# A fused attention and two-MLP kernel: order of the first softmaxes, one weight slice kept on the core, and the pace of two background preparations

## The chip, the cores and the metric

One Trainium2 chip, one of its cores. The metric is the time of one execution in device microseconds; the median of several executions counts. Five engines work side by side, each through its own queue: TensorE (PE in the profile; its weight loads are PEld), VectorE (DVE), ScalarE (ACT), GpSimd (POOL) and SyncE (SP), which here issues all DMA transfers.

## What is computed

Packed attention, then two MLPs over its result, in float32. Batch 8, 8 heads, 576 tokens, head size 64, 32 packing queries; width 512, inner widths 2048 and 1024.

```python
def sm_attn(q, k, v):
    s = q @ k.T / sqrt(64)
    a = exp(s - max(s)); a = a / (sum(a) + 1e-9)
    return a @ v
p_packed = sm_attn(p, k, v)                 # 32 rows a head
x = sm_attn(q, p_packed, p_packed)          # 576 rows a head; heads side by side: 4608 x 512
h = maximum(x @ w_in, 0)                    # 4608 x 2048
y = (h * h) @ w_out                         # 4608 x 512
h = y @ w_in2                               # 4608 x 1024
solu = h * softmax(h)
ln = (solu - mean(solu)) / sqrt(var(solu) + 1e-6) * g_ln
out = ln @ w_out2                           # 4608 x 512
```

The four weight matrices come as float64 and are turned into float32 on the core.

## The kernel before

**Products.** A float32 product is made of three passes of a faster format (`fp32r`): each operand is split into a rounded high part (a ScalarE copy) and the rest (`split_lo`, line 66, a subtraction on VectorE or GpSimd), and high x high, low x high and high x low are added in PSUM.

**First stages (`t` = 0 to 9).** `K0` is a `Pack` (line 164): it computes the packed attention of batches 0 to 3 for one head after the other. `scores` (197), `soft` (212), `transp` (236, which brings the exponentials through PSUM into `eT`; two copies a head, by turns on VectorE and ScalarE), `packed` (248), and `pairs` (262), which leaves for each pair of heads the packed values in `slc` and, split, in `L`. Batches 4 to 7 follow much later as a second `Pack` inside the steps.

**The first MLP's input weights, per batch.** The attention's last product is merged into the weights: a `Unit` (289) takes a 256 x 256 block of `w_in` (slice `s` of 8, head group `g` of 2), decodes it (`Decode`, 119: a ScalarE activation at line 136 and three VectorE instructions at 141, 147 and 149), splits it (`fin`, 295) and multiplies it by `L` (`product`, 304). The result `pw` is split into `pws` (320, 321), stored to DRAM (`store`, 340), and read back batch by batch as a `slot` (`load_slot`, 350). For batch 0 and slices 0 and 1, `product` first calls `first` (325): it computes batch 0's quarter once more by itself (`pd`) and writes the slot straight from PSUM, so that no way over DRAM is needed. `wout_unit` (354) decodes a chunk of `w_out` in the same manner into `woh` and `wol`.

**The second softmax.** `s2_jobs` (367) makes for a batch and a head group the list of jobs that end in `at` (`ah`, `al`): load of the query, scores `s`, transposes, max, subtraction, exponential, sum, normalization, transpose back, split. For batches 0 and 1 VectorE does all but exponential and high copy. For batch 0's group 1 the list comes in two halves of 288 tokens (`parts` = 2), for the others in one.

**Steps.** From `t` = 10 on (`T0`; step `i` = `t` - 10) the main loop (932) runs 256 steps, one for a batch, a half of its tokens and one of 16 chunks of the inner width: `h1` (445) multiplies `slot` by `at` (6 matmuls), ScalarE applies relu and squares, VectorE splits into `ghl`; three or four steps later `ymm` (475) multiplies by `wo` into four PSUM banks `Y` (12 matmuls). The first 32 steps alternate between batches 0 and 1 in blocks; slice `s` serves chunks `2s` and `2s + 1`, so batch 0 needs slice 2 at step 16 and slice 3 at step 18. Beside that, `at_step` (518) holds a table of jobs for each step: loads of slots, begin and decoding of units (`unit_at`, 529; `wout_at`, 541), softmaxes of later batches, the second `Pack`, its units, and from step 137 on the preparation of the second MLP.

**Preparation of the second MLP.** It runs by Strassen-Winograd with seven instead of eight block products (`strassen`, 830). The weights' seven operands are made by `quads` (635) from decoded units (`wi_unit`, `wx_unit`), one unit every `PD` = 5 steps, and stored to DRAM (`wi_d`, `wx_d`). The seven operands of each of the first 14 pairs of token tiles are made by `pre_y` (753), one pair every `RD` = 6 steps from step 138 on, and stored to `yc_d`. At step `t0` = 230 the buffers of these preparations close (`to_w2`, 584), and the operands come back: `load_wi` (591), `fetch_y` (808), and from step 244 on `load_wx` (597) into the buffers that `wo` leaves free. `h2(0)`, the first product of the second MLP, stands at step 249.

**What sets the order.** Matmuls by `mm` and all DMAs are issued in the program's order. The instructions of VectorE, ScalarE and GpSimd are ordered by the framework's scheduler, by the program's order and by its own estimate of when they are ready, except where they are pinned: by `pin`, or, while `strict[0]` is set (steps 138 to 245), all of them.

Of the kernel before, what the change touches and what calls it, by code (L numbers as in the profile page):

```python
# [27 lines left out]
NPRE = 14  # L28
# [8 lines left out]
def build(tc, qT, kT, vP, pT, w_in, w_out, w_in2, w_out2, g_ln, out):  # L37
# [25 lines left out]
    def dma(out, in_):  # L63
        pin(SP.dma_start(out=out, in_=in_))
# [99 lines left out]
    class Pack:  # L164
# [71 lines left out]
        def transp(self, n):  # L236
            t = self.pl.tile([P, KC * P], F32, tag="eT", name="eT", bufs=2) if self.own else t25("2", "eT")
            self.eT[n] = t.rearrange("p (k c) -> p k c", k=KC)
            for a, b in ((0, 3), (3, KC)):
                pt = bank("pt")[:, :(b - a) * P]  # L240
                for c in range(a, b):
                    flip(self.own, pt[:, (c - a) * P:(c - a + 1) * P], self.e1[n % 2][:, c * P:(c + 1) * P], ident)
                if next(TURN["ETC"]) == "A":
                    A.copy(t[:, a * P:b * P], pt)
                else:
                    V.tensor_copy(t[:, a * P:b * P], pt)
# [28 lines left out]


    wo, slot = {}, {}
    T0 = 10
    ring, clock = [0], [0]
    later, soons, lows = [], [], []  # L280

    def soon(fn):
        if strict[0]:
            soons.append(fn)
        else:
            fn()


    class Unit:
        def __init__(self, bg, s, g, pl, bufs):  # L290
            self.bg, self.s, self.g, self.pl, self.done = bg, s, g, pl, False
            self.d = Decode(pl, w_in.rearrange("(k p) c -> p k c", p=P)[:, 2 * g:2 * g + 2, s * 512:(s + 1) * 512],
                            (2, 256), self.fin, bufs)

# [9 lines left out]

        def product(self):
            bg, s, g = self.bg, self.s, self.g
            if bg == 0 and s < 2:
                self.first()
            t = [bank("pw") for _ in range(2)]
            for j in range(2):  # L310
                c = slice(j * 256, (j + 1) * 256)
                for i, (a, x) in enumerate(((0, 0), (1, 0), (0, 1))):
                    for hh in range(2):
                        r = slice(64 * hh, 64 * hh + 64)
                        mm(t[hh][:, c], L[bg, 2 * g + j][r, a, :], self.w[r, x, c], start=(i == 0), stop=(i == 2))
            sb = self.pl.tile([P, 4, 2, 2, P], F32R, tag="pws", name="pws", bufs=2)
            for hh in range(2):
                o = sb.rearrange("p (j h) c l x -> p h j c l x", h=2)[:, hh]
                src = t[hh].rearrange("p (j c x) -> p j c x", j=2, c=2)
                pin(A.copy(o[:, :, :, 0], src))  # L320
                V.tensor_tensor(out=o[:, :, :, 1], in0=src, in1=f(o[:, :, :, 0]), op=ALU.subtract)
            later.append(lambda: self.store(f(sb.rearrange("p h c l x -> p h (c l x)"))))


        def first(self):
            s, g = self.s, self.g
            if (0, s) not in slot:
                new_slot(0, s)
            t = bank("pd")[:, :256]
            for j in range(2):  # L330
                for i, (a, x) in enumerate(((0, 0), (1, 0), (0, 1))):
                    for hh in range(2):
                        r = slice(64 * hh, 64 * hh + 64)
                        mm(t[64 * j + 32 * hh:64 * j + 32 * hh + 32], f(L[0, 2 * g + j][r, a, :32]),
                           f(self.w[r, x, j * 256:(j + 1) * 256]), start=(i == 0), stop=(i == 2))
            o, src = slot[0, s][:, g], t.rearrange("p (c x) -> p c x", c=2)
            pin(A.copy(o[:, :, 0], src))
            V.tensor_tensor(out=o[:, :, 1], in0=src, in1=f(o[:, :, 0]), op=ALU.subtract)

        def store(self, sf):  # L340
            bg, s, g = self.bg, self.s, self.g
            for b4 in range(bg == 0 and s < 2, 4):
                r = slice(32 * b4, 32 * b4 + 32)
                dma(pw_d[4 * bg + b4, s, :, g].rearrange("(h p) c -> p h c", h=4), sf[r])

# [172 lines left out]
    def at_step(i, fn):  # L518
        jobs.setdefault(i if i == "first" else T0 + i, []).append(fn)

# [44 lines left out]
                i = max(i, 9 + 24 * s // 5)  # L565
            at_step(base + i, lambda b=b, s=s: load_slot(b, s))
    for s, (i, k) in enumerate(((None, 4), (None, 6), (11, 12), (15, 16), (25, 26), (29, 30), (39, 40), (43, 44))):
        if i:
            at_step(i, lambda s=s: load_slot(0, s))
        at_step(k, lambda s=s: load_slot(1, s))  # L570

# [125 lines left out]
        unit_at(P2 + 1 + u * 12 // 5, 1, u // 2, u % 2, lambda: X["p"], (3, 2, 2))  # L697
    p1 = P2 + 1 + 36 + 9
    at_step(p1, open_prep)
    PD = 5  # L700
    for u in range(16):
        mk = (lambda u=u: wi_unit(u // 4, u % 4)) if u < 8 else (lambda u=u: wx_unit((u - 8) // 2, u % 2))
        decode_at(p1 + 1 + PD * u, mk)
    t0 = 230
    assert p1 + 1 + PD * 15 + 6 <= t0
    at_step(t0, lambda: W2["dst"].close())
    at_step(t0, lambda: X["yst"].close())
# [39 lines left out]
        return {"11": yl[:, :, :P], "12": yr[:, :, :P], "21": yl[:, :, P:], "22": yr[:, :, P:]}  # L747


    R0, RD = 138, 6  # L750
    assert R0 + RD * (NPRE - 1) >= 213 > R0 + 5 * RD >= 101

    def pre_y(m):
        i0 = R0 + RD * m
# [53 lines left out]
    def fetch_y(i):  # L808
        m = ORDER[i]
        c = places(i)  # L810
        if m < NPRE:
            for j, n in enumerate(AO):
                dma(f(c[n]), yc_d[m][:, j])
            ytl[i] = {n: halves(t) for n, t in c.items()}
            return
        ytl[i] = {n: halves(t) for n, t in c.items()}
        y2 = [p2.tile([P, 2, 256], F32, tag=f"yf{k}", name="yf", bufs=1) for k in range(2)]
        for k in range(2):
            dma(y2[k], y_d[:, 2 * k:2 * k + 2, m * 256:(m + 1) * 256])
        for js in operands(quadrants(*y2), lambda n: (*ytl[i][n], lambda: None), lambda n: V if n in ("22", "12") else G):  # L820
            for fn, *x in js:
                fn(*x)
# [76 lines left out]
        W2["yst"].close()  # L899

    for i in range(2):
        at_step(t0 + 4 + 6 * i, lambda i=i: fetch_y(i))
    for i in range(14):
        at_step(t0 + 1 + i, lambda i=i: load_wi(i))
    at_step(249, lambda: h2(0))


    K0 = Pack(0, era, False)
# [9 lines left out]
    ps1 = {}  # L918
    early = {}
    done = [0]  # L920
    q0 = {}

    def load_q(g):
        if g == 0:
# [7 lines left out]
    for t in range(max(max(j for j in jobs if j != "first"), T0 + N + LAG - 1) + 2):  # L932
        i = t - T0
        clock[0] = t
        if not 1 <= i <= 3:
            for fn in later:
                fn()
            later.clear()
        for n in ((0,), (1,), (2,), (3,), (4, 5), (6, 7))[t] if t < 6 else ():
            K0.load_v(n)  # L940
        if t + 3 < H:
            K0.load_k(t + 3)
        if t + 1 < H:
            K0.scores(t + 1)
        if t == 3:
            load_q(0)
        if t == 5:
            load_q(1)
            for j in jobs.pop("first"):
                j()  # L950
        if t == H:
            ps0_st.close()
            ps1["p"], ps1["st"] = pool("ps1", space=PSUM)
            Y += [ps1["p"].tile([P, HF], F32, name=f"Y{o}") for o in range(4)]
        if 0 <= t - 1 < H:
            K0.transp(t - 1)
        if t + 1 < H:
            K0.soft(t + 1)
        if 0 <= t - 2 < H:
            K0.packed(t - 2)  # L960
        if t in (4, 6, 8, 9):
            K0.pairs(t // 2 - 2 if t < 9 else 3)
        if t < 9:
            products()
        if t == 6:
            for j in s2_jobs(0, 0, q0[0]):
                j()
        if t == 9:
            early[0] = s2_jobs(0, 1, q0[1], 2)
            for j in early[0][:2]:  # L970
                j()
            products()
            for j in early[0][2:9]:
                j()
            open_b()
            early[1] = s2_jobs(1, 0), s2_jobs(1, 1)
            for x in early[1]:
                x.pop(0)()
            x, y = early[1]
            early[1] = x[:4] + [j for z in zip(x[4:], y) for j in z] + y[len(x) - 4:]  # L980
        strict[0] = R0 <= i < 246
        sq = None
        if 0 <= i < N:
            sq = h1(steps[i])
        for fn in soons:
            fn()
        soons.clear()
        if sq and not strict[0]:
            sq[0]()
            sq[1]()  # L990
        for j in jobs.get(t, ()):
            j()
        if sq and strict[0]:
            sq[0]()
        for fn in lows:
            fn()
        lows.clear()
        if sq and strict[0]:
            lows.append(sq[1])
        products()  # L1000
        if i == 0:
            for j in early[0][9:]:
                j()
        if 1 <= i < 6:
            for j in early[1][4 * i - 4:4 * i]:
                j()
        while done[0] < N and done[0] <= i - lag(i):
            ymm(steps[done[0]])
            done[0] += 1
# [120 lines left out]
```

## Time and profile before

| | |
|---|---|
| median of 3 runs | 1218.3 us (1217.76 to 1219.68) |
| the profiled execution's time | 1216.89 us |
| its span, first to last instruction | 1215.1 us |
| busy: TensorE, its weight loads | 1148.2 us (94%), 1055.3 us (87%) |
| busy: VectorE, ScalarE, GpSimd | 879.2, 665.6, 581.8 us (72, 55, 48%) |
| mean granted TensorE clock | 0.983 |

The span is one execution, taken by the hardware profiler. A share of busy time is a mean over stages with different limits, so the rows below go by stretches. An instruction's idle time before it stands in square brackets in the timeline, with what ended it; where several things had to be ready, it is the last one that is named. The granted clock is 1.00 or 0.50 at a time; a stretch shows the mean.

### The profile page before, as it was taken

The numbers are of one execution on the slowest core, as the hardware profiler recorded it, in microseconds if no ns is written. First come the engines' busy times: TensorE is split into PE (matmuls) and PEld (weight loads), VectorE is DVE, ScalarE is ACT, GpSimd is POOL, SyncE is SP. The second block draws the span as 40 slices with busy tenths as digits, with TensorE's granted clock in tenths as the row PEclk, the third lists the DMA queues.
The fourth block names the chain that finished last, engine by engine and source line by source line (L and its number), as shares of the span: only waits on it lengthen the run. The fifth ranks groups of instructions, "written<-read, shape, count | busy, mean of one in ns | idle before, by whom it ended". The sixth has DMA issues, their size and how long they took to land. (4 is left out here: it accounts for less than half of the span.)

```text
span 1215.1 us, 24017 instructions
## 1 busy us (share of the span) xinstructions
PE 1148.2 (94%) x8652; PEld 1055.3 (87%) x8652; DVE 879.2 (72%) x1700; ACT 665.6 (55%) x1505; POOL 581.8 (48%) x591
## 2 busy tenths in 40 slices
PE   6678899999999999999998899999999999999998
PEld 3368899898999998998998899998889899889897
DVE  4787588745326766579877982257989789889886
ACT  3476555344445555566666674435554655655553
POOL 1112254534225544487866781113654764745743
PEclk9988899999999999999999999999999999999999
DMA  9667697655155899789699799653142143223201
GB/s 331 217 198 193 187 300 225 227 203 199 57 198 155 214 290 303 203 308 378 228 393 340 255 368 366 223 171 114 44 144 90 38 143 105 87 83 109 79 23 48
DMA packets 124775, 238.04 MB, mean 196 GB/s; under 512 B 16624, under 2 KB 44272, under 8 KB 124656
## 3 DMA queue, kind: packets, MB, share of 16 engines
q1 hardware_dynamic: 124656, 236.50, 58.4%
q8 instruction: 68, 1.11, 0.4%
q14 instruction: 51, 0.42, 0.1%
HBM read 144.71 MB, written 91.75 MB: 195 GB/s over the span
## 5 line engine op out<-in xcount | busy, mean ns | idle before, releaser
L58 PE MATMUL Y<-ghl,woh 128*128 128x288 f32 x2048 | 467.6, 304 | 13.5 <-DVE ghl L53 6.5
L58 PEld LDWEIGHTS Y<-ghl,woh 128*128 128x128 f32 x2048 | 348.4, 191 | 28.0 <-DVE ghl L53 7.5
L58 PE MATMUL Y<-ghl,wol 128*128 128x288 f32 x1024 | 305.9, 299 | 0.0
L58 PE MATMUL h<-ah,slot 128*128 128x288 f32 x1024 | 215.7, 299 | 18.4 <-ACT ah L432 10.1
L838 PE MATMUL o<-wx,ch 128*128 128x256 f32 x1008 | 191.3, 287 | 5.3 <-DVE ys L855 2.9
L58 PEld LDWEIGHTS Y<-ghl,wol 128*128 128x128 f32 x1024 | 196.1, 192 | 0.0
L1034 POOL TENSOR_TENSOR cl<-raw,ch 128x512 fp32r<-128x512 f32 x100 | 148.4, 1505 | 96.9 <-ACT ch L1033 51.7
L58 PEld LDWEIGHTS h<-ah,slot 128*128 128x128 f32 x1024 | 167.3, 191 | 21.1 <-ACT ah L432 10.5
L469 POOL TENSOR_TENSOR rg<-rg 128x288 f32<-128x288 f32 x128 | 94.0, 736 | 171.7 <-ACT rg L462 157.6
L838 PEld LDWEIGHTS o<-wx,ch 128*128 128x128 f32 x1008 | 160.0, 192 | 12.2 <-DVE ys L855 4.4
L58 PE MATMUL h<-al,slot 128*128 128x288 f32 x512 | 152.3, 297 | 1.5 <-DVE al L67 1.4
L838 PE MATMUL o<-wx,cl 128*128 128x256 f32 x504 | 142.7, 286 | 2.5 <-POOL cl L1034 2.0
L67 DVE TENSOR_TENSOR ghl<-rg,ghl 128x288 fp32r<-128x288 f32 x149 | 79.5, 539 | 81.7 <-POOL rg L469 60.8
L462 ACT ACTIVATE rg<-h 128x288 f32<-128x288 f32 x148 | 60.7, 410 | 105.8 <-PE h L58 105.3
L53 DVE TENSOR_TENSOR ghl<-rg,ghl 128x288 fp32r<-128x288 f32 x107 | 78.0, 742 | 50.5 <-ACT ghl L53 25.3
L1033 ACT CAST ch<-raw 128x512 fp32r<-128x512 f32 x126 | 76.7, 622 | 62.2 <-DVE raw L1039 54.3
L838 PEld LDWEIGHTS o<-wx,cl 128*128 128x128 f32 x504 | 95.9, 191 | 4.9 <-POOL cl L1034 3.0
L58 PEld LDWEIGHTS h<-al,slot 128*128 128x128 f32 x512 | 97.6, 191 | 2.0 <-DVE al L67 2.0
L67 POOL TENSOR_TENSOR ws<-dw,ws 128x512 fp32r<-128x512 f32 x32 | 42.1, 1314 | 109.0 <-ACT ws L298 81.8
L53 ACT ACTIVATE rg<-h 128x288 f32<-128x288 f32 x108 | 44.1, 409 | 88.2 <-PE h L58 85.0
L838 PE MATMUL h<-wi,y 128*128 128x512 f32 x312 | 83.4, 402 | 0.4 <-DVE hs L855 0.3
L1039 DVE TENSOR_TENSOR raw<-raw 128x512 f32<-128x512 f32 x70 | 73.6, 1060 | 9.9 <-POOL cl L1034 5.0
(170 smaller groups left out, 2125.8 us busy)
## 6 DMA issues: line engine op xcount, KB each, us to landing
pw_d<-pws SPq DMA_DIRECT2D x124, 256.0 KB, 4.4
slot<-pw_d SPq DMA_DIRECT2D x62, 512.0 KB, 6.2
yc_d<-yo SPq DMA_DIRECT2D x98, 256.0 KB, 6.2
y<-yc_d SPq DMA_DIRECT2D x92, 256.0 KB, 4.2
raw<-w_in SPq DMA_DIRECT2D x40, 512.0 KB, 6.4
raw<-w_out SPq DMA_DIRECT2D x24, 512.0 KB, 6.2
kf<-kT SPq DMA_DIRECT2D x32, 288.0 KB, 6.2
out<-ys SPq DMA_DIRECT2D x72, 128.0 KB, 1.7
```

The lines of the kernel that those rows point to most:

```text
L53: return (lambda *a, **k: pin(fn(*a, **k))) if strict[0] else fn
L58: pin(PE.matmul(*a, **k))
L67: eng.tensor_tensor(out=lo, in0=x, in1=f(hi), op=ALU.subtract)
L462: A.activation(r, pb[:, :HF], AF.Relu)
L469: G.tensor_tensor(out=gg, in0=r, in1=r, op=ALU.mult)
L838: PE.matmul(bk, x, w[:, y], start=(i == 0), stop=(i == 3 * nk - 1))
L1033: A.copy(c[n][0], x)
L1034: eng.tensor_tensor(out=c[n][1], in0=x, in1=f(c[n][0]), op=ALU.subtract)
L1039: eng.tensor_tensor(out=out, in0=x, in1=y, op=op)
```

## The change

For `K0`'s last three heads both copies of `transp` go to ScalarE. Slice 3 of batch 0 is written from PSUM as slices 0 and 1 are (`FIRST`), and its way over DRAM falls away. At `t` = 9 the second softmax of batch 0's group 1 is written out in one pinned order with `first` of the waiting unit in its midst, ahead of that unit's product; before, its second half came after step 0's jobs. The queries of batch 1 are loaded at `t` = 7 into the buffers of `sums`, and its softmaxes begin at step 0 instead of step 1, four jobs a step as before. `soon` holds back its work only inside the steps.

The units of the second MLP's weights begin every 6 steps (`PD`) instead of 5, the pairs of `pre_y` every 7 (`RD`) instead of 6. `t0` goes from 230 to 241. The input weights are then loaded two a step in the order of their use, the first pair's operands come at `t0` and the second's six steps later, and `h2(0)` goes from step 249 to 252.

```diff
@@ -240,7 +240,7 @@
                 pt = bank("pt")[:, :(b - a) * P]
                 for c in range(a, b):
                     flip(self.own, pt[:, (c - a) * P:(c - a + 1) * P], self.e1[n % 2][:, c * P:(c + 1) * P], ident)
-                if next(TURN["ETC"]) == "A":
+                if next(TURN["ETC"]) == "A" or n > 4 and not self.own:
                     A.copy(t[:, a * P:b * P], pt)
                 else:
                     V.tensor_copy(t[:, a * P:b * P], pt)
@@ -275,12 +275,12 @@
 
 
     wo, slot = {}, {}
-    T0 = 10
+    T0, FIRST = 10, (0, 1, 3)
     ring, clock = [0], [0]
     later, soons, lows = [], [], []
 
     def soon(fn):
-        if strict[0]:
+        if strict[0] and clock[0] > T0:
             soons.append(fn)
         else:
             fn()
@@ -288,7 +288,7 @@
 
     class Unit:
         def __init__(self, bg, s, g, pl, bufs):
-            self.bg, self.s, self.g, self.pl, self.done = bg, s, g, pl, False
+            self.bg, self.s, self.g, self.pl, self.done, self.begun = bg, s, g, pl, False, False
             self.d = Decode(pl, w_in.rearrange("(k p) c -> p k c", p=P)[:, 2 * g:2 * g + 2, s * 512:(s + 1) * 512],
                             (2, 256), self.fin, bufs)
 
@@ -304,7 +304,7 @@
 
         def product(self):
             bg, s, g = self.bg, self.s, self.g
-            if bg == 0 and s < 2:
+            if bg == 0 and s in FIRST and not self.begun:
                 self.first()
             t = [bank("pw") for _ in range(2)]
             for j in range(2):
@@ -323,7 +323,7 @@
 
 
         def first(self):
-            s, g = self.s, self.g
+            s, g, self.begun = self.s, self.g, True
             if (0, s) not in slot:
                 new_slot(0, s)
             t = bank("pd")[:, :256]
@@ -339,7 +339,7 @@
 
         def store(self, sf):
             bg, s, g = self.bg, self.s, self.g
-            for b4 in range(bg == 0 and s < 2, 4):
+            for b4 in range(bg == 0 and s in FIRST, 4):
                 r = slice(32 * b4, 32 * b4 + 32)
                 dma(pw_d[4 * bg + b4, s, :, g].rearrange("(h p) c -> p h c", h=4), sf[r])
 
@@ -565,7 +565,7 @@
                 i = max(i, 9 + 24 * s // 5)
             at_step(base + i, lambda b=b, s=s: load_slot(b, s))
     for s, (i, k) in enumerate(((None, 4), (None, 6), (11, 12), (15, 16), (25, 26), (29, 30), (39, 40), (43, 44))):
-        if i:
+        if i and s not in FIRST:
             at_step(i, lambda s=s: load_slot(0, s))
         at_step(k, lambda s=s: load_slot(1, s))
 
@@ -697,11 +697,11 @@
         unit_at(P2 + 1 + u * 12 // 5, 1, u // 2, u % 2, lambda: X["p"], (3, 2, 2))
     p1 = P2 + 1 + 36 + 9
     at_step(p1, open_prep)
-    PD = 5
+    PD = 6
     for u in range(16):
         mk = (lambda u=u: wi_unit(u // 4, u % 4)) if u < 8 else (lambda u=u: wx_unit((u - 8) // 2, u % 2))
         decode_at(p1 + 1 + PD * u, mk)
-    t0 = 230
+    t0 = 241
     assert p1 + 1 + PD * 15 + 6 <= t0
     at_step(t0, lambda: W2["dst"].close())
     at_step(t0, lambda: X["yst"].close())
@@ -747,8 +747,7 @@
         return {"11": yl[:, :, :P], "12": yr[:, :, :P], "21": yl[:, :, P:], "22": yr[:, :, P:]}
 
 
-    R0, RD = 138, 6
-    assert R0 + RD * (NPRE - 1) >= 213 > R0 + 5 * RD >= 101
+    R0, RD = 138, 7
 
     def pre_y(m):
         i0 = R0 + RD * m
@@ -899,10 +898,11 @@
         W2["yst"].close()
 
     for i in range(2):
-        at_step(t0 + 4 + 6 * i, lambda i=i: fetch_y(i))
+        at_step(t0 + 6 * i, lambda i=i: fetch_y(i))
     for i in range(14):
-        at_step(t0 + 1 + i, lambda i=i: load_wi(i))
-    at_step(249, lambda: h2(0))
+        o = WO.index(("11", "21", "T2", "T3", "T1", "22", "T4")[i // 2])
+        at_step(t0 + 1 + i // 2, lambda i=i, o=o: load_wi(i % 2 * 7 + o))
+    at_step(252, lambda: h2(0))
 
 
     K0 = Pack(0, era, False)
@@ -918,7 +918,7 @@
     ps1 = {}
     early = {}
     done = [0]
-    q0 = {}
+    q0, q1 = {}, {}
 
     def load_q(g):
         if g == 0:
@@ -965,18 +965,25 @@
         if t == 6:
             for j in s2_jobs(0, 0, q0[0]):
                 j()
+        if t == 7:
+            for g in range(2):
+                x = sums()
+                q1[g] = [x[:, :S], x[:, S:]]
+                dma(x.rearrange("p (k c) -> p k c", k=2), qT[1, g])
         if t == 9:
-            early[0] = s2_jobs(0, 1, q0[1], 2)
-            for j in early[0][:2]:
+            x = s2_jobs(0, 1, q0[1], 2)
+            x, y = (x[:2] + x[2:9]), x[9:]
+            u = queue[0]
+            assert u.ready()
+            strict[0] = True
+            for j in (x[0], x[1], x[2], x[3], y[0], y[1], x[4], y[2], u.first, x[5], x[6], x[7], y[3], x[8], y[4], y[5], y[6]):
                 j()
+            strict[0] = False
             products()
-            for j in early[0][2:9]:
-                j()
             open_b()
-            early[1] = s2_jobs(1, 0), s2_jobs(1, 1)
-            for x in early[1]:
-                x.pop(0)()
-            x, y = early[1]
+            x, y = (s2_jobs(1, g, q1[g]) for g in range(2))
+            x.pop(0)()
+            y.pop(0)()
             early[1] = x[:4] + [j for z in zip(x[4:], y) for j in z] + y[len(x) - 4:]
         strict[0] = R0 <= i < 246
         sq = None
@@ -998,11 +1005,8 @@
         if sq and strict[0]:
             lows.append(sq[1])
         products()
-        if i == 0:
-            for j in early[0][9:]:
-                j()
-        if 1 <= i < 6:
-            for j in early[1][4 * i - 4:4 * i]:
+        if 0 <= i < 5:
+            for j in early[1][4 * i:4 * i + 4]:
                 j()
         while done[0] < N and done[0] <= i - lag(i):
             ymm(steps[done[0]])
```

## Rows read from the trace of the kernel before

**Rows 1.** Stretches: start:end, length, busy us (instructions) an engine, clock, DMA share, GB/s.
```profile
498.30:551.30 53.00, 53.00 (x397) 53.00 (x396) 38.67 (x51) 33.01 (x89) 40.68 (x46) 1.00 0.79 280
551.30:613.00 61.70, 60.05 (x441) 57.52 (x440) 55.81 (x77) 41.63 (x112) 47.95 (x52) 1.00 0.84 301
613.00:676.00 63.00, 58.14 (x412) 55.53 (x412) 50.19 (x76) 40.07 (x108) 41.91 (x48) 0.97 0.94 352
676.00:705.00 29.00, 24.87 (x173) 24.62 (x174) 27.41 (x44) 18.47 (x51) 20.79 (x24) 0.94 0.82 278
```
**Rows 2.** Stretches around steps 0, 8 and 18: PE, PEld, DVE, ACT, POOL, clock, DMA.
```profile
55.80:62.50 6.70, 0.03 (x1) 0.00 (x0) 6.70 (x18) 3.96 (x10) 2.50 (x2) 0.80 0.59 138
62.50:66.60 4.10, 4.01 (x25) 1.96 (x27) 2.92 (x6) 2.01 (x5) 0.94 (x2) 0.50 0.95 337
...
92.20:97.40 5.20, 5.20 (x28) 4.97 (x28) 3.05 (x4) 2.25 (x6) 2.75 (x2) 0.50 0.32 104
...
132.60:138.30 5.70, 5.70 (x24) 5.70 (x25) 0.47 (x2) 1.86 (x4) 0.00 (x0) 0.50 0.73 274
```
**Rows 3.** TensorE's waits over the span: us in total, times, longest us.
```profile
PE Y L58 <- DVE ghl L53: 6.5, 4, 2.7
PE h L58 <- DMA slot<-pw_d: 4.4, 1, 4.4
...
PE h L58 <- DVE pws L321: 3.0, 2, 2.4
```
**Rows 4.** TensorE's timeline: start, us, engine line operation count [idle before].
```profile
62.50 0.85 PE L58 MATMUL h<-ah,slot 128*128 128x288 f32 x2 [6.68 <-ACT ah L432]
...
68.03 1.95 PE L58 MATMUL pd<-ws,L 64*32 64x256 f32 x24
...
89.73 0.53 PE L58 MATMUL h<-ah,slot 128*128 128x288 f32 x2 [3.38 <-ACT ah L432]
91.64 0.61 PE L58 MATMUL h<-al,slot 128*128 128x288 f32 x1 [1.38 <-DVE al L67]
```
**Rows 5.** VectorE's timeline ahead of step 0.
```profile
54.79 0.42 DVE L338 TENSOR_TENSOR slot<-pd,slot 128x256 fp32r<-128x256 f32 x1 [1.96 <-ACT slot L337]
...
56.22 1.28 DVE L321 TENSOR_TENSOR pws<-pw,pws 128x512 fp32r<-128x512 f32 x2
57.46 1.08 DVE L141 TENSOR_SCALAR dw<-dw 128x512 uint32<-128x512 uint32 x1
```
**Rows 6.** VectorE's timeline ahead of step 8.
```profile
89.15 1.35 DVE L141 TENSOR_SCALAR dw<-dw 128x512 uint32<-128x512 uint32 x1
...
91.88 0.68 DVE L149 SCALAR_TENSOR_TENSOR dw<-raw,dw 128x512 uint32<-128x512 uint32 x1
```
**Rows 7.** VectorE alone, from step 0's softmax to step 8: busy us, clock, DMA.
```profile
51.60:92.00 40.40, 34.31 (x73) 0.88 0.60 183
```
**Rows 8.** VectorE's groups in 560 to 740 us: busy us, mean ns | idle before.
```profile
L53 DVE TENSOR_TENSOR op<-dw,op 128x256 fp32r<-128x256 f32 (+1 forms) x39 | 28.4, 770 | 0.0
L53 DVE SCALAR_TENSOR_TENSOR dw<-raw,dw 128x512 uint32<-128x512 uint32 x24 | 25.0, 1042 | 0.8
L53 DVE TENSOR_TENSOR dw<-dw 128x256 f32<-128x256 f32 (+1 forms) x21 | 15.5, 737 | 0.3
L53 DVE TENSOR_TENSOR yo<-yf,yo 128x256 fp32r<-128x256 f32 x21 | 14.2, 674 | 11.9 <-ACT yo L53 11.9
L53 DVE TENSOR_SCALAR dw<-dw 128x512 uint32<-128x512 uint32 x12 | 9.0, 750 | 3.8 <-ACT dw L53 3.8
```
**Rows 9.** TensorE's timeline of the second MLP's first product, `h2(0)`: its first and last.
```profile
787.42 2.97 PE L838 MATMUL h<-wi,y 128*128 128x512 f32 x12
...
796.44 0.85 PE L838 MATMUL h<-wi1T,y 128*128 128x512 f32 x3
```
**Rows 10.** A stretch in which `wi` and `y` are loaded; columns as in rows 1.
```profile
750.00:760.00 10.00, 10.00 (x78) 10.00 (x77) 1.88 (x5) 4.43 (x12) 1.33 (x2) 1.00 1.04 411
```
**Rows 11.** The page's line on all DMA packets.
```profile
DMA packets 124775, 238.04 MB, mean 196 GB/s; under 512 B 16624, under 2 KB 44272, under 8 KB 124656
```

## The prediction

> **What bounds the kernel now.** I read the engines' totals first, then stretches, then TensorE's own waits, and last single instructions. TensorE is busy for nearly all of the span, so only two things can be won: its idle time, and work done while the granted clock is 0.50 (1.2 instead of 2.4 GHz). A plain step (18 matmuls of 288 columns) shows its price where nothing waits: 397 matmuls in 53.0 us [rows 1], 2.40 us a step.
>
> The losses that this change can reach lie in two places. In the first twenty steps TensorE stands for 6.7 us ahead of step 0 and then runs 4.1 us at half clock; it stands again for 3.4 us ahead of step 8 and runs 5.2 us at half clock; and it stands for 4.4 us ahead of step 18, with 5.7 us at half clock [rows 2 to 4]. Each time the clock falls beside the idle stretch and comes back after some microseconds of work. In steps 160 to 215 (551 to 705 us) the three stretches have 1.65, 4.86 and 4.13 us without a matmul, 10.6 together, and clocks of 0.97 and 0.94 [rows 1]: another 0.03 x 58.1 + 0.06 x 24.9 = 3.2 us. That is about 14 us. The waits there are on VectorE's `ghl` [rows 3].
>
> **First softmaxes.** Step 0 waits for the second group's attention weights, `ah`. VectorE's row shows why it is late: between the slot's subtraction at 54.79 and step 0's matmul at 62.50 it does two `pws` subtractions (1.28) and the three instructions of a w_out decode (1.08, and twice 0.68, as the same instructions take later) [rows 5, 6]. That is 3.7 us that is not softmax. The diff writes the order out: both halves' max, subtraction and exp, the PSUM slice, then the rest, and only then the products' evictions and the decode. So step 0's matmul can start some 3.7 to 5 us earlier (the upper end counts the exponentials, which now leave ScalarE ahead of a cast and a decode). Its half-clock stretch, 4.1 us of work at half speed, is worth another 2 us if the shorter pause doesn't bring the clock down.
>
> This doesn't arrive whole. VectorE has 34.3 us of work between 51.6 and 92 us, 85% of that time [rows 7], and step 8 needs nearly all of it: both softmaxes of batch 1, the decodes of w_out chunk 2 and w_in slice 2. What can wait past step 8 is the decode of chunk 3, now ahead of the last `al`: 1.35 + 0.68 + 0.68 = 2.7 us (the middle one is like the last) [rows 6]. That leaves 31.6 us, plus about 1 us for the wait on the PSUM slice that stays in VectorE's queue (1.96 now [rows 5]), plus some 2 us of other idle time: 51.6 + 34.6 = 86.2 us, where the matmul of step 8 goes on at about 91.6 now [rows 4]. So the pause moves from step 0 to step 8, and the gain there is about 5.5 us; bounds 2 (idle time as now, only the decode saved) and 11 (both pauses gone and both half-clock stretches with them). The half-clock stretch behind step 8 I leave as it is.
>
> The three `eT` copies that go from VectorE to ScalarE take about 0.5 us each from an engine that is full there and give it to one that has room; I take 0 to 0.5 us, inside the bounds.
>
> The queries of batch 1 now load at stage 7 into the `ys` buffers instead of after the era's pool closes. On SP's queue they stand behind the stores of the first product and ahead of those of the next; their buffers are free once the last scores and the first query matmul have run. I cost this at nothing; if a buffer came late, the first product's later stores would wait for it.
>
> **Fourth slice from PSUM.** Slice 3 of batch 0 is no longer stored, read back (512 KB) and waited for: the 4.4 us wait of step 18 is on exactly such a load [rows 3], and the 5.7 us at half clock behind it cost 2.85. Against it stand two more groups of `pd` matmuls. One takes 1.95 us at full clock [rows 4], so 3.9 for two, in TensorE's own queue and thus in full on the path. Their evictions (a ScalarE copy and the 0.42 us subtraction of [rows 5]) lie beside matmuls. Net 4.4 + 2.85 - 3.9 = 3.4 us gained; from -1 (another load, or slice 2's, is late in its place and the clock still falls) to 3.4. I take 3. The 2.4 us wait at step 14 on a `pws` eviction [rows 3] is an accident of the order of unpinned work; it may go or double: 0 plus or minus 2.
>
> First part: 5.5 + 3 = 8.5 us gained, bounds 2 and 16.
>
> **Operands of y and second MLP's weights.** From step 138 on, the order on each engine is the program's. The pairs go from six steps to seven, the units from five to six. In 560 to 740 us VectorE spends 28.4 + 25.0 + 15.5 + 9.0 = 77.9 us on the units and 14.2 on the pairs [rows 8]; a sixth of one and a seventh of the other are 15.0 us of 180, 8.3%. In 551 to 705 VectorE is busy for 55.8 + 50.2 + 27.4 = 133.4 us [rows 1]. Less 8.3% that is 122.3, over the 139.7 us that are left if the whole loss goes: 87.5%. At 90% (551 to 613) TensorE lost 2.7% of its time; at 73% (498 to 551) nothing [rows 1]. By a line between them 87.5% loses 2.3%, 3.2 us, and I add 1 us of half clock. So of 14 us some 10 are gained. Bounds: 4, if the stalls come from single steps in which a unit's combinations, a softmax and a pair meet (they still meet, every 42 steps instead of 30), and 14. GpSimd and ScalarE lose the same shares of their part. What moves to steps 230 to 241 meets a VectorE that is nearly free there.
>
> **What is paid for it.** The room for the second MLP's input weights opens at step 241 instead of 230. Until step 248 SP issues, in this order, the first pair's operands (7 x 256 KB), fourteen weights of 512 KB in the order of their use, ten halves of output weights and the second pair's operands: 13.6 MB. The products with them stand behind step 252 instead of 249. In the time of before, the first stands at 787.4 and the last weight is used 9.0 us later, at 796.4 [rows 9]; three steps on that is 803.6. Step 241 begins 8 steps and the 0.8 us of one `h` ahead of 787.4, at 767.4, so loading starts at about 769, when the last stores have landed. At 411 GB/s [rows 10] 13.6 MB take 33.2 us: 802 and a start-up of 2 to 3 us, so just at the edge. I take 1.5 us lost, from 0 to 6.
>
> The Trainium skill's page "DMA: Bandwidth & Descriptors" (section "Bandwidth") gives about 358 GB/s as what HBM grants a core; by that the load would take an estimated 38 us and the loss would be some 5 us. The 411 GB/s that this trace shows for the same weights speak against it here.
>
> **Sum.** 8.5 + 10 - 1.5 = 17 us. The profiled execution took 1216.9 us for its span of 1215.1, 1.4 under the median of 1218.3, so its microseconds count as they are: 1218.3 - 17 = 1201.
>
> **Rivals.**
> VectorE stays full from step 0 to step 8, and the order changes only who waits: the first part gives 2 for the softmaxes and 3 for the slice. 1218.3 - 5 - 10 + 1.5 = 1205. For it speaks the 85% of [rows 7], against it that a part of this work isn't wanted by then. Chance 0.18.
> The stalls of steps 160 to 215 are peaks, not load, and only 5 us of 14 go: 1218.3 - 8.5 - 5 + 1.5 = 1206. For it: 613 to 676 lost the most at a VectorE share of only 80% [rows 1]. Chance 0.17.
> The change doesn't do what it says, since decodes are unpinned and get in between the softmaxes all the same: nothing for the softmaxes, 1218.3 - 3 - 10 + 1.5 = 1207. Chance 0.10.
> Slower than before: the weights of the second MLP come late. The place is the sixth and seventh product behind step 252, where TensorE's queue stands still, as each wants its weight in order. The price is the time of 13.6 MB beyond the 35 to 36 us that there are. It outweighs the 18.5 us of gains from 54 us of loading on, below 250 GB/s; at the mean of the whole kernel, 196 [rows 11], it takes 69 us: 33 lost, 1233. Against it: 411 GB/s for the same tiles. Chance 0.06.
> Better than forecast: both pauses and both stretches at half clock go, and nearly all of the later loss: 1218.3 - 15 - 13 + 0 = 1190. Chance 0.09.
>
> **How the numbers follow.** The forecast, 1201, has 0.40. The range reaches from 1190, the best case, to 1211, which takes in the three milder cases and some sum of two of them; what is left out is the slower case and the sums of three. Measurements of this kernel can tell about 0.2% (2.4 us) from no change. All cases but one lie over 7 us below 1218.3; two of the milder ones together with the 6 us of late weights come near it. Faster 0.89, same 0.05, slower 0.06.
>
> **What would show it.** Right: step 0's first `h` group ends its wait some 4 us earlier; step 8 still waits, for a weight or for `al`; the wait on `slot` from `pw_d` is gone and two `pd` groups stand at steps 12 and 13; waits on `ghl` in the middle fall below 4 us in all; loads of `wi` run at 370 GB/s or more and end within some 3 us of their use. Wrong: decodes between the two exponentials and `al`; a wait of over 6 us on `wi`; new waits on `slot` 2 or on raw weights, from work that now runs earlier than its loads.

## The result, and the profile after

| | before | after |
|---|---|---|
| median | 1218.0 us of 4 runs | 1207.8 us of 4 runs (1204.4 to 1208.4) |
| profiled execution, its span | 1216.9, 1215.1 us | 1207.7, 1205.9 us |
| mean granted TensorE clock | 0.983 | 0.987 |

The ratio is 0.9913, interval 0.9893 to 0.9933: the changed kernel is faster by 10.6 us, 8 to 13. The forecast was 17 us, a time of 1201. Gains here and below are worked out from the ratio; differences of the medians are up to 1.3 us off them. Where the time went is seen from the time at which TensorE begins the same step in both profiled executions:

| begin of | before | after | after is |
|---|---|---|---|
| step 0 (its first `h`) | 55.2 | 53.0 | 2.2 ahead |
| step 0, behind its pause | 62.5 | 60.5 | 2.0 ahead |
| step 1 (its first `h`) | 70.8 | 74.6 | 3.7 behind |
| step 14 | 116.8 | 126.2 | 9.4 behind |
| step 24 | 151.9 | 152.6 | 0.7 behind |
| step 48 | 223.4 | 223.1 | 0.3 ahead |
| step 160 | 551.3 | 551.5 | 0.2 behind |
| step 215 | 704.9 | 693.1 | 11.8 ahead |
| step 249 | 786.6 | 776.0 | 10.6 ahead |
| step 255 | 810.9 | 801.5 | 9.3 ahead |

So the whole gain lies in steps 160 to 215, and the first part of the change, for which 8.5 us were forecast, brought nothing. The 2.0 us ahead at step 0 were there before its pause began; at step 1 they are lost. The 9.4 us behind at step 14 are in part the two added `pd` groups (4.0 us) and in part order: in the changed kernel all of the stretches at half clock lie ahead of that step, before two of the four lie behind it. From step 14 to step 24 the changed kernel then takes 26.4 us for the same 204 matmuls that took 35.1, and doesn't stand at all.

The stretches that answer to [rows 1] and [rows 2] (start:end, length, busy us and instructions of PE, PEld, DVE, ACT, POOL, clock, DMA share, GB/s), from the changed kernel; the first is at half clock, the second holds the pause ahead of step 1:

```profile
57.10:67.30 10.20, 5.99 (x37) 3.13 (x39) 9.29 (x22) 4.95 (x11) 2.56 (x2) 0.50 0.02 5
71.60:74.60 3.00, 0.08 (x3) 0.05 (x1) 0.79 (x2) 1.07 (x2) 0.00 (x0) 0.93 0.97 358
...
551.80:602.90 51.10, 50.79 (x375) 48.72 (x374) 42.01 (x64) 32.69 (x86) 33.86 (x40) 1.00 0.69 247
602.90:665.90 63.00, 61.34 (x450) 59.05 (x449) 52.03 (x71) 39.86 (x109) 42.90 (x48) 1.00 0.95 348
665.90:693.50 27.60, 27.32 (x203) 27.08 (x203) 26.52 (x43) 20.55 (x56) 19.80 (x23) 1.00 0.74 253
```

In the middle, 551.8 to 693.5, TensorE stands for 0.3 + 1.7 + 0.3 = 2.3 us instead of 10.6, and the clock is 1.00 throughout.

TensorE's waits from 50 to 145 us of the changed kernel (us in total, times, longest), which answer to [rows 3]:

```profile
PE h L58 <- ACT ah L53: 6.9, 1, 6.9
PE h L58 <- DVE pws L321: 2.9, 1, 2.9
PE pw L58 <- DVE pws L321: 2.9, 2, 2.0
PE h L58 <- ACT ah L432: 1.3, 1, 1.3
PE pw L58 <- DVE slot L338: 1.3, 1, 1.3
PE h L58 <- DVE al L67: 1.1, 1, 1.1
PE h L58 <- DVE al L53: 0.8, 1, 0.8
PE pw L58 <- POOL ws L67: 0.7, 1, 0.7
PE pd L58 <- ACT rg L462: 0.5, 1, 0.5
PE pw L58 <- ACT ws L298: 0.4, 1, 0.4
```

The wait on a `slot` from `pw_d` is gone, and the waits ahead of step 8 are half as long (1.3 and 1.1). The wait on `ah` ahead of step 0 is as long as it was, and those on `pws` have grown from 2.9 to 5.8 us. Together these rows are 18.8 us. Before, the same stretch had the waits of [rows 4], 6.7 + 3.4 + 1.4, with 4.4 and 2.4 of [rows 3] and two small ones (0.5 and 0.2): 19.0. The waits have moved; their sum is the same.

The waits from 498 to 745 us, of the changed kernel:

```profile
PE Y L58 <- DVE ghl L53: 1.6, 2, 1.3
PE Y L58 <- ACT ys L53: 0.6, 2, 0.3
PE h L58 <- DVE t L53: 0.3, 1, 0.3
```

That is 2.5 us. Before, it was 6.5 on `ghl` [rows 3] and three more:

```profile
PE Y L58 <- DVE ys L53: 2.6, 2, 2.3
PE h L58 <- DVE t L53: 1.0, 1, 1.0
PE Y L58 <- ACT ghl L53: 0.5, 1, 0.5
```

together 10.6.

### The profile page after: what moved, and what is told of

It reads as the page before. It is cut to its first block, busy times and chain, and to the rows that moved or that the text cites. A ratio compares the mean times of both kernels' runs of the same rounds, so it can differ in the third digit from the quotient of the medians.

```text
span 1205.9 us, 24131 instructions
## 1 busy us (share of the span) xinstructions
PE 1149.1 (95%) x8700; PEld 1053.9 (87%) x8700; DVE 881.5 (73%) x1699; ACT 664.8 (55%) x1510; POOL 579.0 (48%) x591
## 5 line engine op out<-in xcount | busy, mean ns | idle before, releaser
L53 DVE TENSOR_TENSOR ghl<-rg,ghl 128x288 fp32r<-128x288 f32 x107 | 78.2, 743 | 29.6 <-ACT ghl L53 15.7
L53 ACT ACTIVATE rg<-h 128x288 f32<-128x288 f32 x108 | 44.3, 410 | 85.2 <-PE h L58 80.6
```

Of the source, the lines that this page charges most:

```text
L53: return (lambda *a, **k: pin(fn(*a, **k))) if strict[0] else fn
```

## Experiments

All were timed in five rounds against the kernel before on the same chip, where its median was 1216.6 to 1218.0 us. "Early part" means the first softmaxes, the queries, the copies and the slice; "late part" the paces of units and pairs and what follows from them.

### The late part alone

```diff
+    PD = 6
+    t0 = 241
+    R0, RD = 138, 7
...
+        at_step(t0 + 6 * i, lambda i=i: fetch_y(i))
...
+    at_step(252, lambda: h2(0))
```

> The later part of the change alone: units every 6 steps, pairs every 7, operands back at step 241, first product at step 252; the early part as before. Theory A (the whole gain is the later part's: step 212 starts 11.5 us earlier in the changed kernel, of which the early part holds about 0, and 1.3 are paid at step 252): 1218 - 10.5 = 1207.5 us, the same as the whole change within 2 us. Theory B (the early part carries a part of it, hidden by what the trace shows later): 1210 or more.

1205.8 us, ratio 0.9906 (0.9887 to 0.9926): 11.4 us gained, as theory A had it. Its waits from 498 to 745 us are line for line those of the whole change. The late part carries the whole gain.

### The early part alone

The change with the hunks from `PD` to `at_step(252, ...)` undone.

> The early part alone: softmaxes in the written order, fourth slice from PSUM, copies on ScalarE; the later part as before. Theory A: 1218 within 2 us. Theory B (the prediction's sum, 8.5 us): 1210 us.

1216.7 us, 0.9999 (0.9986 to 1.0012): nothing. So the question became which of its pieces gives and which takes.

### Only the fourth slice

```diff
-    T0 = 10
+    T0, FIRST = 10, (0, 1, 3)
...
-        if i:
+        if i and s not in FIRST:
```

> Only the fourth slice from PSUM, the softmaxes as before. Theory A (the slice saves the 4.4 us wait and its half-clock stretch of 2.9, and costs two groups of pd matmuls of 1.95): 1215 us, 3 less than before. Theory B (another late load or a wait of the added evictions takes the place of the wait): 1218 within 1 us.

1213.2 us, 0.9964 (0.9951 to 0.9977): 4.4 us gained. By the begin of steps, steps 12 and 13 take 1.6 and 3.4 us longer, and steps 14 to 19 together 8.8 less: net 3.8. TensorE's timeline in step 13:

```profile
117.90 0.35 PE L58 MATMUL pw<-ws,L 64*128 64x256 f32 x1 [1.28 <-DVE slot L338]
```

Behind the `pd` group, the product's first `pw` waits 1.28 us for the slot's subtraction to release a PSUM bank: the evictions do not lie beside matmuls in full.

### Only the softmaxes, queries and copies

```diff
-    T0, FIRST = 10, (0, 1, 3)
+    T0, FIRST = 10, (0, 1)
```

on the early part alone.

> Only the softmaxes' order with the earlier loads of the queries and the copies on ScalarE; slice 3 over DRAM as before. Theory A (decodes still stand between the pinned softmax instructions, and the first product's evictions, now behind them, make the third product wait for a pws buffer): 1221 us, 3 slower than before, with a pause of about 7 us ahead of step 0 and a new one ahead of step 1. Theory B (the order gains what was predicted, and it is the slice's added matmuls that eat it): 1213 us.

1221.2 us, 1.0033 (1.0018 to 1.0048): 4.0 us slower than before. The waits from 50 to 140 us that lead:

```profile
PE h L58 <- ACT ah L53: 6.9, 1, 6.9
PE h L58 <- DMA slot<-pw_d: 6.5, 1, 6.5
PE h L58 <- DVE pws L321: 4.8, 2, 2.4
```

Theory A holds. Step 0's pause is not shorter, the wait on slice 3 grows from 4.4 to 6.5, and a second wait on `pws`, ahead of step 1, joins the one of step 14. In this piece the forecast had +5.5 with a lower bound of 2; it is -4.0. That cancels the slice's +4.4.

### The decodes of w_out two steps later

If decodes between the softmaxes hold step 0 up, it must start earlier without them. On the whole change:

```diff
-            i = -4 + fc
+            i = -2 + fc
```

in `wout_at` (`w_out` chunks 0 and 1).

> The whole change, with the decodes of w_out's chunks 0 and 1 two steps later (from steps -1 and 0 to 1 and 2). Theory A (decodes that the scheduler puts between the pinned instructions are part of the late weights: 0.42 + 0.69 + 0.68 us of VectorE stand between the second subtraction and the first transpose): the pause ahead of step 0 falls from 6.9 to about 5 us, the time by 2, to 1205. Theory B (VectorE fills idle time with them, and the pause is made by the pinned chain itself, which waits for the slot's copy behind the second exponential): the pause stays within 0.5 us.

1211.4 us, 0.9953 (0.9934 to 0.9972): 4 to 5 us slower than the whole change. TensorE's waits from 50 to 100 us:

```profile
PE Y L58 <- ACT woh L358: 5.8, 2, 5.0
PE h L58 <- ACT ah L53: 3.8, 1, 3.8
...
PE Y L58 <- POOL wol L67: 2.1, 2, 1.4
```

Step 0's pause falls from 6.9 to 3.8 us, so the decodes have a part in it (theory B is out), but the time went the other way than theory A said. Steps 4 and 5 now wait 7.9 us for `woh` and `wol`. That is an exchange, but no sign that VectorE was full. Between step 0 and step 1 it is busy for half of the time (start:end, length, VectorE's busy us, clock, DMA):

```profile
62.00:72.00 10.00, 5.11 (x10) 0.96 0.63 185
```

The decode begins only at 74.22, behind step 1, where it now stands. The traced execution took 1207.3 us, the least of nine; what makes the others 3 to 8 us longer it doesn't show.

### The first unit's evictions ahead of the softmaxes

On the whole change, the unit's product with its evictions stands where `u.first` stood:

```diff
- y[2], u.first, x[5]
+ y[2], products, x[5]
...
-            products()
```

(the first two lines shortened).

> The whole change, with the first unit's whole product and its evictions at the place of the PSUM slice, ahead of the softmax's second half, instead of behind all of it. Theory A (the evictions behind the softmax delay the product's stores, SP's queue behind them, and the third product's buffer: the new pauses at steps 1 and 9): the 2.9 us wait of step 1 is gone, the stores are issued some 6 us earlier, the pause ahead of step 0 grows by up to 1.4 us, and the time falls by 3 to 5 us, to 1203 to 1205. Theory B (the new pause comes from batch 1's first scores, which now stand ahead of step 1): the wait of step 1 stays.

1206.1 us, 0.9905 (0.9885 to 0.9926), within the interval of the whole change; theory A's 3 to 5 us don't show in the median. TensorE's first `h` of steps 0 and 1 [idle before it, with what ended it]:

```profile
63.46 0.85 PE L58 MATMUL h<-ah,slot 128*128 128x288 f32 x2 [8.96 <-ACT ah L53]
...
73.86 0.53 PE L58 MATMUL h<-ah,slot 128*128 128x288 f32 x2 [0.28 <-DVE pws L321]
```

and SyncE's queue:

```profile
59.55 1.53 SPq L64 DMA_DIRECT2D pw_d<-pws  x3
```

The stores go out 6.7 us earlier, and step 1's wait of 2.9 us is gone: the late eviction was its cause. But step 0 waits 2.1 us longer, for the evictions now stand in its softmax. In the traced execution (1202.9 us, 3.3 under the median) the steps from 0 to 24 take 95.6 us instead of 99.6: there less came back than went.

### Batch 1's softmaxes from step 1 again

On the whole change:

```diff
-            if 0 <= i < 5: early[1][4 * i:4 * i + 4]
+            if 1 <= i < 6: early[1][4 * i - 4:4 * i]
```

(shortened).

> The whole change, with batch 1's softmaxes one step later, from step 1 as before. Theory A (the cost lies in batch 0's written-out order, whose product is evicted late): the pauses at steps 0 and 9 stay, 1207 us, as the whole change. Theory B (it lies in batch 1's earlier softmaxes, whose scores take two PSUM banks ahead of step 1): the pause of 2.9 us at step 1 is gone, 1204 us or less.

1206.0 us, 0.9907 (0.9889 to 0.9924): like the whole change. The wait on `pws` is still there, now behind step 1's `h` and ahead of the scores of batch 1:

```profile
PE s L58 <- DVE pws L321: 2.0, 1, 2.0
```

So beginning batch 1's softmaxes a step earlier is not what costs. That leaves the order at `t` = 9, the copies, which cost nothing that could be seen in the last experiment below, and the earlier loads of the queries, which were not tried alone.

### The late part with the slice, softmaxes as before

Both pieces that gained, on the kernel before.

> The later part and the fourth slice, the softmaxes as before. Theory A (the parts add up: 10.8 and 3.4 us): 1202.5 us. Theory B (they interact): further off than 2 us.

1202.9 us, 0.9887 (0.9867 to 0.9907): 13.8 us faster than before. The pieces add up to 11.4 + 4.4 = 15.8, within what the intervals of 1.6 and 2.4 us leave open. This version, which leaves the softmaxes alone, is clearly faster than the kernel before. Against the changed one (0.9913) it lies 3 us lower by the ratios and 5 by the medians, but the intervals overlap by 1.4 thousandths: likely, not shown.

### The same, with the decodes of w_out later

The edit in `wout_at` on that version.

> The later part and the fourth slice, the softmaxes in the order of before, and the decodes of w_out's chunks 0 and 1 two steps later. Theory A (in the order of before the 2.4 us of one decode on VectorE's chain delay step 0, so taking them away helps there, and part of it is lost again at step 8, which needs the same VectorE work): 1201 us, a pause of about 4.3 us ahead of step 0. Theory B (VectorE's sum up to step 8 decides): 1202.5 within 1 us.

1206.3 us, 0.9913 (0.9891 to 0.9934), 3 us slower than without the edit; neither theory had that. TensorE's waits from 50 to 100 us:

```profile
PE h L58 <- ACT ah L432: 4.5, 1, 4.5
PE Y L58 <- ACT woh L358: 2.5, 2, 2.4
PE Y L58 <- POOL wol L67: 2.1, 2, 1.1
PE h L58 <- DMA slot<-pw_d: 1.7, 1, 1.7
```

With the softmaxes as before it is the same exchange: 2.2 us off step 0's pause, 4.6 more at steps 4 and 5, and at step 8 1.7 for a slot in place of 4.8 for `ah` and `al`. The decode, put at a later step, comes too late for steps 4 and 5.

### The same, with the units at five steps; with the pairs at six

```diff
-    PD = 6
+    PD = 5
```

> Later part and fourth slice, but only the pairs slower (seven steps), the units every five as before. Theory A (VectorE's load makes the stalls of steps 160 to 215, and the units are 77.9 us of it in 560 to 740, the pairs 14.2): most of the later part's gain is lost, 1210 us or more, waits on ghl of over 5 us. Theory B (GpSimd's long subtractions for the pairs, 85.4 us in the same stretch, make them): 1204 us.

1208.2 us, 0.9929 (0.9913 to 0.9944): 5 us of that version's gain are lost, between the two theories, and the waits on `ghl` are 1.8 us where theory A had over 5. The two largest waits from 498 to 760 us:

```profile
PE Y L58 <- ACT ys L53: 2.7, 1, 2.7
PE Y L58 <- DVE ghl L53: 1.8, 2, 0.9
```

The counterpart:

```diff
-    R0, RD = 138, 7
+    R0, RD = 138, 6
```

> Later part and fourth slice, but only the units slower (six steps), the pairs every six as before. Theory A (VectorE's load, mostly the units): 1204 us, within 2 us of both together. Theory B (GpSimd's load by the pairs): 1210 us or more.

1202.6 us, 0.9878 (0.9858 to 0.9898): no loss is seen. The begin of step 215 less that of step 160, in the traced executions with the slice, tells more than the times (versions with the same paces agree there within 0.4 us with pairs at seven and units at six, and within 1.3 with six and five):

| pairs every | units every | steps 160 to 215, us |
|---|---|---|
| 6 | 5 | 153.2 |
| 7 | 5 | 146.6 |
| 6 | 6 | 144.0 |
| 7 | 6 | 141.5 |

So either pace alone brings more than half of the 11.7 us, the units' more than the pairs', and with the units at six the pairs' seventh step is still worth 2.5 us there, which is too little for the times to show.

### The same, with the copies on ScalarE

```diff
-                if next(TURN["ETC"]) == "A":
+                if next(TURN["ETC"]) == "A" or n > 4 and not self.own:
```

> Later part and fourth slice, softmaxes as before, and the three eT copies on ScalarE. Theory A (the copies make step 0 begin earlier, 45.5 us behind the first matmul instead of 47.9 to 49.1): 1201 us, some 2 us under the same kernel without them, as VectorE ends its chain earlier too. Theory B (step 0's own wait hides it, or the order of the first stages is another cause of the earlier begin): 1202.9 within 1 us.

1200.5 us (1197.4 to 1207.1), 0.9873 (0.9846 to 0.9899). That is the lowest median, but its interval and that of the version without the copies overlap, and step 0's pause is 6.7 us as before. The copies' worth stays open: 1.7 us by the ratios, with noise of some 4 us to either side.

## Why the prediction was right and wrong

**First softmaxes: wrong, in the step "step 0's matmul can start some 3.7 to 5 us earlier".** TensorE's timeline of the changed kernel (steps 0 and 1):

```profile
60.50 0.85 PE L58 MATMUL h<-ah,slot 128*128 128x288 f32 x2 [6.88 <-ACT ah L53]
...
74.55 0.85 PE L58 MATMUL h<-ah,slot 128*128 128x288 f32 x2 [2.92 <-DVE pws L321]
```

The pause is 6.88 us where [rows 4] have 6.68. VectorE's timeline shows what stood in the way:

```profile
54.04 1.39 DVE L53 TENSOR_TENSOR t<-t,mx 128x288 f32<-128x288 f32 x1
...
55.83 0.46 DVE L53 TENSOR_TENSOR t<-t,mx 128x288 f32<-128x288 f32 x1
56.21 0.42 DVE L141 TENSOR_SCALAR dw<-dw 128x512 uint32<-128x512 uint32 x1
56.66 0.69 DVE L147 SCALAR_TENSOR_TENSOR dw<-raw,dw 128x512 uint32<-128x512 uint32 x1
...
57.96 0.68 DVE L149 SCALAR_TENSOR_TENSOR dw<-raw,dw 128x512 uint32<-128x512 uint32 x1
...
59.50 0.48 DVE L53 STREAM_TRANSPOSE aT<-t 128x288 f32<-128x288 f32 x1
```

Lines shown as L53 are the pinned ones. The order that the diff writes out holds among them alone. The decode of `w_out` (L141, L147, L149) is not pinned, and its three instructions, 1.8 us, lie between the softmax's own; the next chunk's follow at 60.24. The `pws` subtractions did move behind, but the decode that the forecast took to go with them did not. This is the rival that had a chance of 0.10, "decodes get in between all the same", and the first sign of being wrong that the forecast named. Its time, 1207, is the measured one by luck: it had 0 for the softmaxes, 3 for the slice and 8.5 for the rest, where -4.0, 4.4 and 11.4 were measured.

The decodes are not the whole of it. In the fifth experiment, without them, step 0 goes on at 58.66 instead of 60.50 and its pause is 3.1 us shorter. But 1.2 us of these are TensorE's, which comes to the pause that much later there, and the subtraction that takes 1.39 us at 54.04 takes 0.46 (see the last section).

**A wait that no rival had.** The products' evictions now stand behind both softmaxes on VectorE. The forecast noted the subtractions only as 1.28 us that leave the way of step 0, and asked what would come late behind them for the queries alone. SyncE's queue tells it, first before, then after:

```profile
57.53 1.53 SPq L64 DMA_DIRECT2D pw_d<-pws  x3
59.11 1.19 SPq L64 DMA_DIRECT2D raw<-w_out  x1
```

```profile
66.26 1.53 SPq L64 DMA_DIRECT2D pw_d<-pws  x3
67.83 1.21 SPq L64 DMA_DIRECT2D raw<-w_out  x1
```

The stores are issued 8.7 us later, and the loads of raw weights behind them with them: from 57.1 to 67.3 us the DMA engines all but stand still, at 5 GB/s. There are two `pws` buffers, so the eviction of the third product waits for a store to land, on ScalarE:

```profile
73.19 1.07 ACT L320 CAST pws<-pw 128x512 fp32r<-128x512 f32 x2 [3.16 <-DMA pw_d<-pws]
```

and TensorE's step 1 for that eviction, 2.92 us. With the evictions ahead again, this wait is gone. A third `pws` buffer was not tried.

**The pause "moves to step 8": wrong in its place.** At step 8, 4.8 us of waits became 2.4 (`ah` 1.3, `al` 1.1). The forecast had VectorE at 31.6 us of work and 3 us of idle time from 51.6 on. Measured, up to the last `al` of step 8 (columns as in the fifth experiment):

```profile
51.60:92.90 41.30, 34.69 (x70) 0.83 0.45 147
```

That is 34.7 us of work, no less than before, and 6.6 idle; one wait of 3.3 us, for the eviction that waits for the store, is half of this. So both terms were too small. The rival "VectorE stays full, and the order changes only who waits" isn't shown either. Later decodes did bring as much wait a few steps on, but with VectorE half idle in between, and with the evictions first less came back than went.

**The sum of the first part.** From the first `h` of step 0 to that of step 24 both kernels run the same matmuls but for two more `pd` groups in the changed one (2.05 and 1.95 us). First before, then after:

```profile
55.17:151.88 96.71, 77.56 (x546) 68.35 (x545) 70.09 (x132) 60.40 (x141) 23.02 (x19) 0.88 0.64 187
```

```profile
52.96:152.58 99.62, 80.93 (x594) 69.70 (x593) 76.18 (x137) 60.88 (x144) 23.24 (x20) 0.88 0.58 172
```

TensorE stands for 18.7 us instead of 19.2 and works for 80.9 instead of 77.6; at half clock both run 18.8 us of matmuls. So the waits give back 0.5 us, the matmuls cost 3.4 more, and 2.2 us ahead become 0.7 behind. The 2.2 us are no gain to count on: with batch 1's softmaxes as before, the same work ahead of step 0 brought its first `h` at 55.9. At step 48, 0.3 us ahead, it is nothing, as for the early part alone. The half-clock stretch behind step 0 was to be the 2 us that come on top; it has 6.0 us of matmuls instead of 4.0. The first part's lower bound, 2, wasn't the sum of its terms' (2, -1 and -2), which is -1; measured was 0.

**Fourth slice: right.** Forecast 3 us, bounds -1 and 3.4; measured 4.4 (2.8 to 6.0), or 3.8 by the steps, a little over the upper bound. "Their evictions lie beside matmuls" was too kind, by 1.3 us for a PSUM bank; the "accident", step 14's wait on `pws`, was gone in the same run and made up for it.

**Middle: right in place and size; the mechanism is shown in part.** The forecast had 10 of 14 us; between steps 160 and 215, 11.8 were gained. Of the waits 8.1 went, and with them the two stretches at half clock (3.4 us each, so 3.4 us of time): 11.5. Wrong is the line by which VectorE's share was turned into a loss. The rows under it spoke against it: at 80% TensorE lost 7.7%, at 95% 14% [rows 1]. Now the share is 82, 83 and 96%, by the stretches above, no lower than before in the last two, and at 96% TensorE loses 1%. So a mean share does not set the loss, the rival "peaks, not load" had a point, though not in its price, and that the line led to 10 us is luck in part.

Nor does the gain go by VectorE's sum. The pairs were 2 of the 15 us of its relief, and yet they alone bring 6.6 of the 11.7 us (table above). That a slower pace takes the stalls away is shown. Whether by VectorE, by GpSimd's subtractions for the pairs, or by fewer steps in which a unit, a softmax and a pair meet, no run parts.

**What is paid late: right in its term, not in all.** Forecast 1.5 us; the step that holds the product lasts 13.4 us (step 252) against 12.1 before (step 249), 1.3 more. Another 1.2 us go between steps 215 and 249, 0.3 of it a wait; the forecast had the work that moves there at nothing. What the rest is stays open. TensorE waits for the last weights only briefly, for 0.4 and 0.3 us:

```profile
793.07 0.94 PE L837 MATMUL h<-wi0T,y 128*128 128x512 f32 x3 [0.43 <-DMA wi0T<-wi_d]
```

while they load, as one stretch shows, at

```profile
780.00:790.00 10.00, 10.00 (x58) 8.85 (x57) 2.84 (x7) 3.19 (x7) 2.01 (x3) 1.00 1.05 411
```

411 GB/s again, as in [rows 10]. The 358 GB/s of the Trainium skill's page "DMA: Bandwidth & Descriptors" (section "Bandwidth"), which that section gives a core when both cores of a pair stream, would have made it an estimated 5 us. This kernel runs on one core, and its trace decides for 411.

**In sum**, the forecast was 8.5 + 10 - 1.5; the separate runs show 0 and 11.4. The error of 7 us is that of one piece, the softmaxes: -4.0 instead of +5.5. The slice's 1.4 us more and the late part's 2.9 more take part of it back. The range reached to 1211 for cases in which the softmaxes give little or nothing, and the time lies in it; that they could cost something was in none of them.

## What to carry to other kernels

A written-out order binds only the instructions that are in it: list what else is ready on that engine in those microseconds, and count it in. When work is put behind other work, follow what it frees and issues: its store, what is queued behind that store, and the next user of its buffer. And a mean busy share tells neither how much idle time an engine will have in its new order nor what stalls it causes: look at the single waits, and try each pace and each piece by itself.

## What the runs showed of the hardware

The same subtraction of 128x288 takes 0.46 us at 55.83 and 1.39 us at 54.04 (above). GpSimd's instruction beside the slow one runs from 53.86 to 55.13:

```profile
53.86 1.27 POOL L67 TENSOR_TENSOR ws<-dw,ws 128x512 fp32r<-128x512 f32 x1 [0.53 <-ACT ws L298]
```

The slow one ends at 55.43, 0.3 us behind it. In the execution with the decodes of `w_out` two steps later, GpSimd's instruction runs from 55.07 to 56.34, and the same subtraction has VectorE to itself:

```profile
53.71 0.46 DVE L53 TENSOR_TENSOR t<-t,mx 128x288 f32<-128x288 f32 x1
```

The Trainium skill's page "SBUF — State Buffer" (section "SBUF: two separate sides") says that VectorE, in an instruction with two SBUF inputs, and GpSimd take turns on a shared port, each for a whole instruction. These rows agree. No run moved the GpSimd instruction alone, so that the port is the cause is likely and not shown.

A pause of 2.9 us ahead of step 1 was followed by 3.4 us at half clock from 74.2 on, with 3.05 us of matmuls in it. The 1.5 us that this costs come on top of the pause.
